# x ahead of the weight bits, a first stage on column halves, and two weight parts converted by VectorE and GpSimd

## The chip, the cores and the metric

The kernel runs on one core of a Trainium2 chip. The core has TensorE (PE in the profile; its weight loads are PEld), VectorE (DVE), ScalarE (ACT), GpSimd (POOL), and SyncE (SP), which here only issues DMAs. Sixteen DMA engines move data between HBM and the on-chip memory SBUF; TensorE writes into a second on-chip memory, PSUM, of eight banks. The metric is the device time of one execution in microseconds (us); lower is better. Times named "before" are for the kernel without the change.

## The reference

The reference filters a sequence in the frequency domain and puts the result through a two-layer network with a hard-swish:

```python
# x: (8, 3008, 256) float32; filt_r, filt_i: (1505, 256) float32
X = np.fft.rfft(x, axis=1)
F = (filt_r + 1j * filt_i)[None, :, :]
y = np.fft.irfft(X * F, n=3008, axis=1).astype(np.float32)
t = y.reshape(8 * 3008, 256)
h = t @ w_in                                  # w_in: (256, 2048)
g = h * np.clip(h + 3.0, 0.0, 6.0) / 6.0
out = (g @ w_out).astype(np.float32)          # w_out: (2048, 256)
```

Both weights come as 8-byte floating-point numbers. [...]

## The kernel before, in words

**The transform.** 3008 is 47 times 64, and the transform is done in stages of small matrix products. For every batch: a first stage over 47 rows, a second stage (`b_unit`) over 64, the product with the filter (`f_unit`), the way back in two stages (`bi_unit`, then `n_five`, `n_unit`, or `n_first` and `direct` for the very first tokens). Between the stages the data changes its layout. Batches 1 to 7 go through HBM for that (`z_tmp`, `g_tmp`), and their work is spread over the main stage, in which the two weight products (`plain_up` and `plain_down` in the first block of 512 tokens, `up_1` to `up_5` and `down` in the others) fill TensorE. Batch 0 is different: it has to be done first, before the main stage has anything to work on, and it has its own path.

**Batch 0, first stage.** x of batch 0 is loaded by six DMAs (`x0_load`, line 406) into the upper end of the tile `w_all`, which later holds the weights. `x0` is seen as 32 columns j of 256 values. `a0_unit(j)`, called eight times, takes four j; for each half `dh` of the 256 values it makes four products into one PSUM bank, with 128 columns of x as the stationary operand and the 128 columns of the table `start` as the moving one, of which 96 (4 times KH) are then copied out. The copies (`copy`, lines 413 and 415) go to `zt(0)` by ScalarE and to `zt(1)` by VectorE, save for j of 8 and 12, where ScalarE does both. `bank(0)` hands out four PSUM banks in turn.

**Batch 0, second stage.** The loop over c from 0 to 5 is the heart of the change's neighbourhood. `turn(c)` transposes with TensorE and copies with ScalarE. Each round has two units i (2c and 2c+1): `b_unit` is two products on TensorE, `f_unit` three VectorE operations that read the product in PSUM and a filter tile in SBUF. After the round's units come `turn(c + 1)`, `bi_unit(0, 2c - 2)` with two ScalarE copies (line 587) and `g_store(0, 2c - 2)` (line 631): two DMAs issued by GpSimd itself, in the order of its other work. The copies of `bi_unit` go to a buffer that a store reads: units 0, 4 and 8 use the pool `t1p` with two buffers (the tile `y0` of the last round takes one of them between units 4 and 8), units 2 and 6 the single buffer of `t3p`. In the last round `g0_first` issues the stores of unit 8 on ScalarE's and SyncE's queues (line 625). `first_load` (line 663) reads back what the stores wrote, in two parts; `direct` (line 732) and `n_first` make the first tokens from it.

**The order of DMAs.** Loads are issued by SyncE in the order in which the program calls them, and no more than some eight are under way at once. `table_load(0, c)` loads the filter rows and the table of round c (five DMAs, 0.8 MB); rounds 0 and 1 have their own tiles, rounds 2 to 5 go into space that x0 leaves free after the first stage. `load_bits(n)` loads the raw words of weight parts up to part n - 1 (one DMA, 512 KB each). `wi` is a table that `bi_unit` reads.

**The conversion of a weight part.** `w_abs(i)` is a pair of ScalarE operations (lines 323 and 324): the absolute value of the upper word into a tile `high`, and the lower word as a scaled float. `w_conv(i)` is three VectorE operations on the upper word (lines 333, 335, 337), or four where `w_abs` was not called. `w_conv_2(i)` multiplies, adds, and masks tiny numbers, three VectorE operations (lines 354 or 356, 358, 361; line 349 too without `w_abs`). Part 0 is converted in the first stage, after `a0_unit(4)`; parts 1, 2 and 3 after the second stage (`convert(3)`), with `w_abs(3)` behind `n_first`; the other twelve in halves in the first block of the main stage (`convert_half`), each in a step of its plan.

**Order of instructions.** The program order is the order on every engine (`manual_schedule`); semaphores are set where one engine's data is another's input or where a buffer is reused.

Of the kernel before, what the change touches and what calls it, by code (L numbers as in the profile page):

```python
# [10 lines left out]
FP32 = mybir.dt.float32  # L11
I32 = mybir.dt.int32
AXT = mybir.ActivationFunctionType
ALU = mybir.AluOpType
# [15 lines left out]
KH = 24  # L30
X0, XR = 16, 112
NF = N // 2 + 1
P = 128
# [5 lines left out]
HC = NC // 2  # L39
# [6 lines left out]
FB = 2  # L46
# [137 lines left out]
def kernel(  # L184
# [9 lines left out]
    nc = tc.nc  # L194
# [5 lines left out]
    wi_d = nc.inline_tensor(wi_np, name="wi_t").ap()  # L200
# [10 lines left out]
    def pool(name, bufs, **kw):  # L211
        return ctx.enter_context(tc.tile_pool(name=name, bufs=bufs, **kw))
# [4 lines left out]
    sp = pool("sp", 2)  # L217
# [3 lines left out]
    rp = pool("rp", 2)  # L221
# [3 lines left out]
    op = pool("op", 2)  # L225
# [12 lines left out]
    wi = const.tile([P, 4, NC], FP32, name="wi")  # L238
# [10 lines left out]
    st = {}  # L249

    def raw(src, row, ap):
        return bass.AP(tensor=src.tensor, offset=src.offset + row * D, ap=ap)


    def table_load(b, c):
        if b == 0 and c >= FB:

            at = x0_at(1536 * (c - FB), 1536)
            t, wb = at[:, 0:1024].rearrange("p (k d) -> p k d", k=TC), at[:, 1024:].rearrange("p (k m) -> p k m", k=TC)
        else:  # L260

            t, wb = ft[(b * NT + c) % FB], wa[:, ds(c % FB * TC * P, TC * P)].rearrange("p (k m) -> p k m", k=TC)
        st["ft", b, c] = t
        if b:

            for src, p0 in ((filt_r, 0), (filt_i, HALF)):
                for r in range(2):
                    o = p0 + 32 * r
                    nc.sync.dma_start(t[o:o + 16, :, :].rearrange("p k d -> p (k d)"),
                                      raw(src, c * TC + NA * r, [[2 * NA * D, 16], [1, TC * D]]))  # L270
                    nc.sync.dma_start(t[o + 16:o + 32, :, :],
                                      raw(src, NA * (2 - r) - c * TC, [[2 * NA * D, 16], [-D, TC], [1, D]]))
            return
        for src, p0 in ((filt_r, 0), (filt_i, HALF)):
            nc.sync.dma_start(t[p0:p0 + 32, :, :].rearrange("p k d -> p (k d)"),
                              raw(src, c * TC, [[NA * D, 32], [1, TC * D]]))
            nc.sync.dma_start(t[p0 + 32:p0 + 64, :, :], raw(src, NA - c * TC, [[NA * D, 32], [-D, TC], [1, D]]))
        nc.sync.dma_start(wb, wb_d[:, ts(c, TC), :])
        st["wb", b, c] = wb
# [10 lines left out]
    def w_part(i):  # L290
        i = PART[i]
        p = i // 2
        if i % 2 == 0:
            cols = ts(p, 256)
            src = moe_w_in[:, cols].bitcast(I32)
            return src.rearrange("(a p) d -> p a d", p=P), w_in[p][:, 0:4, :].rearrange("p (a j) m -> p a (j m)", a=2)
        src = moe_w_out[ts(p, 2 * P), :].bitcast(I32)
        return src.rearrange("(a p) d -> p a d", p=P), w_out[p][:, 0:4, :].rearrange("p (a j) m -> p a (j m)", a=2)
# [18 lines left out]
        q.dma_start(t.rearrange("p (a d) -> p a d", a=2), w_part(i)[0])  # L317
        st["bits", i] = t

    def w_abs(i):  # L320
        words = st["bits", i].rearrange("p (n two) -> p n two", two=2)
        st["high", i] = sp.tile([P, 512], FP32, name="s1")
        nc.scalar.activation(out=st["high", i], in_=words[:, :, 1].bitcast(FP32), func=AXT.Abs)
        nc.scalar.activation(out=words[:, :, 0].bitcast(FP32), in_=words[:, :, 0].bitcast(mybir.dt.uint32), func=AXT.Copy, scale=2.0 ** -32)


    def w_conv(i):
        words = st.pop(("bits", i)).rearrange("p (n two) -> p n two", two=2)
        lo, hi = words[:, :, 0], words[:, :, 1]
        big, rest = (yp.tile([P, 2, D], FP32, name="y").bitcast(I32).rearrange("p a n -> p (a n)") for j in range(2))  # L330
        v = nc.vector
        st["conv", i] = big, rest, lo, hi
        v.tensor_scalar(out=big, in0=hi, scalar1=3, scalar2=0x3FFFFFFF,
                        op0=ALU.logical_shift_left, op1=ALU.bitwise_and)
        v.scalar_tensor_tensor(out=big, in0=hi, scalar=top_c, in1=big,  # L335
                               op0=ALU.bitwise_and, op1=ALU.bitwise_or)
        v.tensor_scalar(out=rest, in0=big, scalar1=23, scalar2=23,
                        op0=ALU.logical_shift_right, op1=ALU.logical_shift_left)
        if ("high", i) not in st:
            v.tensor_scalar(out=lo, in0=lo, scalar1=9, scalar2=0x3F800000,  # L340
                            op0=ALU.logical_shift_right, op1=ALU.bitwise_or)

    def w_conv_2(i):
        big, rest, lo, hi = st.pop(("conv", i))
# [55 lines left out]
    def x0_at(o, n):  # L400
        return w_all.rearrange("p a b c m -> p (a b c m)")[:, ds(NP * 14 * P - HC * D + o, n)]

    x0 = x0_at(0, HC * D).rearrange("p (j d) -> p j d", d=D)
# [4 lines left out]
    def zt(dh):  # L408
        return (xn.rearrange("p a c n -> p (a c n)"), xs.rearrange("p i j d -> p (i j d)"))[dh]

    def copy(dve, to, ps):
        if dve:
            nc.vector.tensor_copy(out=to, in_=ps)
        else:
            nc.scalar.activation(out=to, in_=ps, func=AXT.Copy)

    def a0_unit(j):
        for dh in range(2):
            ps = bank(0)
            for u in range(4):  # L420
                nc.tensor.matmul(ps[:, ts(u, P)], x0[0:XR, j + u, ts(dh, P)], st["start"][0:XR, ts(1, P)],
                                 start=True, stop=True)
            copy(dh and j not in (8, 12), zt(dh).rearrange("p (n j) -> p j n", j=HC)[:, j:j + 4, :],
                 ps.rearrange("p (j n) -> p j n", j=4)[:, :, 0:4 * KH])

    def turn(c):
# [139 lines left out]
    def y_unit(b, i):  # L566
        s1, s2 = st["y", b, i]
        if b == 0 and i % 2 == 0:
            st["y0"] = t1p.tile([P, 2, 2, D], FP32, name="t1")
        y = yp.tile([P, 2, D], FP32, name="y") if b else st["y0"][:, i % 2, :, :]  # L570
        re, im = slice(0, HALF), slice(HALF, P)
        nc.vector.tensor_tensor(out=y[re], in0=s1[re], in1=s1[im], op=ALU.subtract)
        nc.vector.tensor_tensor(out=y[im], in0=s2[re], in1=s2[im], op=ALU.add)
        st["y", b, i] = y
# [62 lines left out]
    for b in range(B):  # L637
# [4 lines left out]
        n = 0  # L642
# [120 lines left out]
    def strips(ps, w, x, **kw):  # L763
        for o in range(0, P, STRIP):
            nc.tensor.matmul(ps[ds(o, STRIP)], w[:, ds(o, STRIP)], x, skip_group_check=True, **kw)  # L765
# [214 lines left out]
    with tc.manual_schedule():  # L980
# [17 lines left out]
        def load_bits(most):  # L998
            nonlocal loaded
            while loaded < most and w_before(loaded) < done:  # L1000
                w_load(loaded, nc.sync)
                loaded += 1

        def convert(n):
            nonlocal done
            for i in range(n):
                w_conv(done)
                w_conv_2(done)
                done += 1
# [10 lines left out]
            load_bits(NCONV)  # L1020

        nc.scalar.activation(out=zero[:, 0:1], in_=half_c, func=AXT.Copy)
        nc.scalar.dma_start(wi, wi_d)
        ps = psU.tile([P, 512], FP32, name="al")

        def keep_warm(n):
# [1 line left out]
                nc.tensor.matmul(ps, zero[:, P:2 * P], zero, start=True, stop=True)  # L1028

        keep_warm(2)  # L1030
        for j, n, bits in (0, 4, 0), (4, 4, 0), (8, 8, 1), (16, 8, 1), (24, 4, 1), (28, 4, 1):
            x0_load(j, n)
            load_bits(bits)
        table_load(0, 0)
        load_bits(2)
        table_load(0, 1)
        for j in range(0, HC, 4):
            a0_unit(j)
            convert(j == 4)
        nc.gpsimd.memset(t4, 0.0)  # L1040
        for c in range(FB, NT):
            table_load(0, c)
        last = x0_at(HC * D - 2048, 3 * ND)
        nc.sync.dma_start(last, direct_d[:, 0:3, :].rearrange("p k n -> p (k n)"))
        load_bits(3)
# [5 lines left out]
        for c in range(NT):  # L1051
            for i in (2 * c, 2 * c + 1):
                b_unit(0, i)
                f_unit(0, i)
                if c == NT - 1:
                    y_unit(0, i)
            if c + 1 < NT:
                turn(c + 1)
            if c:
                bi_unit(0, 2 * c - 2)  # L1060
                (g0_first if c == NT - 1 else lambda i: g_store(0, i))(2 * c - 2)
            if c == 4:
                first_load(0, KH - 3 * TC)
        first_load(KH - 3 * TC, KH - TC)
        for i in 1, 2:
            w_abs(i)
        direct(NU - 2)
        direct(NU - 1)

# [8 lines left out]
            x_load(1, c)  # L1078
            load_bits(7 + c)
        w_abs(3)  # L1080
        convert(3)

        def wai_load():
            nc.sync.dma_start(wa[:, 528:], wa_d[:, 528:])
# [32 lines left out]
        for i in range(2, len(chunks)):  # L1117
# [7 lines left out]
            s0, s1 = ((k - 1) * NP + s for s in steps)  # L1125
# [63 lines left out]
        for i in range(len(items) + 1):  # L1189
            up = i < len(items)  # L1190
            k, p = items[min(i, len(items) - 1)]
# [98 lines left out]
```

## Time and profile before

| What | Value |
|---|---|
| time, median of 3 runs (lowest to highest) | 2609.06 us (2608.47 to 2609.44) |
| the profiled execution: span from first to last instruction | 2607.0 us |
| the same execution's own time | not listed apart from its span; the median stands 2.06 us above it |
| PE busy | 2591.8 us, 99% |
| DVE busy | 2053.9 us, 79% |
| ACT busy | 1295.6 us, 50% |
| POOL busy | 486.7 us, 19% |
| mean granted TensorE clock | 1.000 |
| first stage of batch 0, PE (L421) | 6.6 to 22.1 us |
| first product of the main stage (L765) | 64.2 us |

A line of the timeline or of a group names the engine, the source line (L421), the operation, the tiles it writes and reads, the shape, and how many records of it there are. A matrix product of 32-bit floats leaves two records. An entry in brackets is the time for which the engine stood idle before it, with the engine or DMA it had waited for. The chain of waits is followed back from the last instruction: at each step to what released it.

### The profile page before, as it was taken

The numbers are of one execution on the slowest core, as the hardware profiler recorded it, in microseconds if no ns is written. First come the engines' busy times: TensorE is split into PE (matmuls) and PEld (weight loads), VectorE is DVE, ScalarE is ACT, GpSimd is POOL, SyncE is SP. The second block draws the span as 40 slices with busy tenths as digits, with TensorE's granted clock in tenths as the row PEclk, the third lists the DMA queues.
The fourth block names the chain that finished last, engine by engine and source line by source line (L and its number), as shares of the span: only waits on it lengthen the run. The fifth ranks groups of instructions, "written<-read, shape, count | busy, mean of one in ns | idle before, by whom it ended". The sixth has DMA issues, their size and how long they took to land.

```text
span 2607.0 us, 86613 instructions
## 1 busy us (share of the span) xinstructions
PE 2591.8 (99%) x37708; PEld 2051.0 (79%) x37708; DVE 2053.9 (79%) x3611; ACT 1295.6 (50%) x2677; POOL 486.7 (19%) x711
## 2 busy tenths in 40 slices
PE   8999999999999999999999999999999999999999
PEld 6487777878778787788877888777877778888887
DVE  7978868888788877888778887788877888766666
ACT  4554454545545455444554444545445454455554
POOL 2242021121211202111031210311113120111110
PEclk9999999999999999999999999999999999999999
DMA  8732234112241132411224112331123321110000
GB/s 247 224 92 81 59 101 119 54 33 87 74 123 54 33 87 78 119 54 37 83 83 114 54 38 82 89 108 54 54 66 91 106 57 49 50 44 24 20 22 26
DMA packets 130834, 200.32 MB, mean 77 GB/s; under 512 B 21602, under 2 KB 97472, under 8 KB 130262
## 3 DMA queue, kind: packets, MB, share of 16 engines
q1 hardware_dynamic: 115165, 150.12, 20.4%
q0 software_dynamic: 14720, 44.16, 6.1%
q8 instruction: 296, 4.85, 0.8%
q14 instruction: 84, 0.69, 0.1%
q10 hardware_dynamic: 569, 0.50, 0.1%
HBM read 122.43 MB, written 83.98 MB: 79 GB/s over the span
## 4 chain that ended last, share of the span: by engine, by line
PE 94%; DVE 3%; DMA 2%; POOL 1%; issue 0%; ACT 0%; SPq 0%; POOLq 0%; DVEq 0%; ACTq 0%
PE po L765 43%; PE al L765 24%; PE be L765 18%; PE psn L705 2%; PE psf L540 1%; PE psf L481 1%; PE psf L600 1%; PE be L600 1%; POOL w_all L369 1%; PE be L481 1%; DVE g L818 1%; DMA g_tmp<-t 1%; PE psf L765 0%; DMA ft<-in_filt_i_dram 0%; DVE y L335 0%
## 5 line engine op out<-in xcount | busy, mean ns | idle before, releaser
L765 PEld LDWEIGHTS po<-w_all,g 128*64 128x64 f32 x20808 | 1232.5, 137 | 247.0 <-issue 12.4
L765 PE MATMUL po<-w_all,g 128*64 128x128 f32 (+1 forms) x20808 | 1407.0, 274 | 1.4 <-DVE g L818 0.7
L813 ACT ACTIVATE r<-h,half_c 128x512 f32<-128x512 f32 x736 | 531.0, 722 | 346.7 <-DVE h L794 334.7
L765 PE MATMUL al<-xt,w_all 128*64 128x256 f32 x4416 | 664.0, 379 | 0.4 <-POOL w_all L369 0.3
L818 DVE SCALAR_TENSOR_TENSOR g<-r,h 128x512 f32<-128x512 f32 x736 | 536.2, 730 | 144.6 <-ACT r L813 129.2
L765 PE MATMUL be<-xt,w_all 128*64 128x256 f32 x2944 | 442.6, 379 | 0.0
L794 DVE TENSOR_TENSOR h<-be,s 128x512 f32<-128x512 f32 x368 | 253.8, 690 | 131.3 <-PE be L765 102.2
L760 POOL TENSOR_TENSOR xt<-xn 128x256 f32<-128x256 f32 x184 | 150.7, 838 | 890.3 <-ACT xn L687 890.3
L765 PEld LDWEIGHTS be<-xt,w_all 128*64 128x64 f32 x2944 | 211.3, 137 | 106.5
L765 PEld LDWEIGHTS al<-xt,w_all 128*64 128x64 f32 x4416 | 278.9, 137 | 1.7 <-POOL w_all L369 1.4
L808 ACT ACTIVATE h<-al 128x256 f32<-128x256 f32 x368 | 141.4, 384 | 273.2 <-PE al L765 272.4
L826 DVE TENSOR_TENSOR g<-g 128x512 f32<-128x512 f32 x367 | 261.4, 712 | 12.6
L799 DVE TENSOR_TENSOR h<-al,s 128x256 f32<-128x256 f32 x368 | 156.0, 424 | 135.6 <-PE al L765 130.5
L789 ACT ACTIVATE s<-al 128x256 f32<-128x256 f32 x368 | 141.6, 385 | 207.2 <-PE al L765 207.1
L765 PE MATMUL al<-xn,w_all 128*64 128x256 f32 (+1 forms) x1536 | 240.1, 393 | 1.1 <-DVE g L818 0.7
L765 PE MATMUL be<-xn,w_all 128*64 128x256 f32 (+1 forms) x1536 | 236.4, 388 | 0.0
L780 ACT ACTIVATE s<-be 128x256 f32<-128x256 f32 x368 | 141.4, 384 | 170.1 <-PE be L765 170.1
L825 DVE TENSOR_TENSOR g<-g 128x256 f32<-128x256 f32 x367 | 165.5, 451 | 12.6
L779 ACT ACTIVATE s<-al 128x256 f32<-128x256 f32 x368 | 141.5, 384 | 59.1 <-PE al L765 59.1
L831 DVE TENSOR_TENSOR g<-g 128x256 f32<-128x256 f32 x367 | 161.7, 441 | 2.4
L765 PEld LDWEIGHTS be<-xn,w_all 128*64 128x64 f32 x1536 | 110.3, 137 | 62.3 <-issue 7.4
L506 POOL DMA_DIRECT2D z_tmp<-t x144 | 72.0, 508 | 321.4 <-ACT s L780 296.0
(162 smaller groups left out, 1766.6 us busy)
## 6 DMA issues: line engine op xcount, KB each, us to landing
t<-g_tmp SPq DMA_DIRECT2D x184, 120.0 KB
t<-z_tmp SPq DMA_DIRECT2D x42, 512.0 KB
g_tmp<-t POOLq DMA_DIRECT2D x68, 256.0 KB, 4.3
z_tmp<-t POOLq DMA_DIRECT2D x120, 144.0 KB, 3.7
o_tmp<-o SPq DMA_DIRECT2D x46, 256.0 KB
xs<-in_x_dram SPq DMA_DIRECT2D x60, 192.0 KB
ft<-in_filt_r_dram SPq DMA_DIRECT2D x168, 64.0 KB
ft<-in_filt_i_dram SPq DMA_DIRECT2D x168, 64.0 KB
```

The source lines that it names most:

```text
L760: nc.gpsimd.tensor_tensor(out=o, in0=x0, in1=x1, op=op_)
L765: nc.tensor.matmul(ps[ds(o, STRIP)], w[:, ds(o, STRIP)], x, skip_group_check=True, **kw)
L779: nc.scalar.activation(out=s[:, 0, :], in_=al, func=AXT.Copy)
L780: nc.scalar.activation(out=s5, in_=be[:, 1, :], func=AXT.Copy)
L789: nc.scalar.activation(out=s[:, 1, :], in_=al, func=AXT.Copy)
L794: nc.vector.tensor_tensor(out=st["h"][0].rearrange("p (a n) -> p a n", a=2), in0=be, in1=s, op=ALU.add)
L799: nc.vector.tensor_tensor(out=st["h"][1][:, 256:512], in0=al, in1=s5, op=ALU.add)
L813: nc.scalar.activation(out=r, in_=st["h"][i], func=AXT.Relu, bias=half_c, scale=1.0 / 6.0)
L818: nc.vector.scalar_tensor_tensor(out=st["g", k, p][:, o:o + 2, :].rearrange("p a n -> p (a n)"), in0=st["r", i], scalar=1.0, in1=st["h"][i ...
L825: v.tensor_tensor(out=g[:, G1, :], in0=g[:, G3, :], in1=g[:, G22, :], op=ALU.add)
L826: v.tensor_tensor(out=g[:, G3:G2 + 1:2, :], in0=g[:, G3:G1 + 1, :], in1=g[:, G11:G11 + 1, :].broadcast_to([P, 2, 256]), op=ALU.subtract)
L831: nc.vector.tensor_tensor(out=g[:, G4, :], in0=g[:, G12, :], in1=g[:, G2, :], op=ALU.subtract)
```

## The change

Three things change. First, the loads: all six DMAs of x go first, then the tables of rounds 0 and 1, then part 0's bits, then `wi` (on SyncE's queue, no longer ScalarE's); part 1's bits go behind table 3. Second, `a0_unit` uses `strips`: each product is made as two, with 64 stationary columns each, and the moving operand is cut to the 96 columns that are copied out; VectorE makes all copies of the second half. Third, parts 0 and 1 are no longer converted in the first stage and after the second, but in rounds 1 and 3 of the second stage: ScalarE's pair, VectorE's three operations, and a new function `w_conv_2g` with four GpSimd operations in place of VectorE's three. Their tile `high` comes from another pool. `convert(3)` becomes `convert(2)`.

```diff
-    def w_abs(i):
+    def w_abs(i, early=False):
         words = st["bits", i].rearrange("p (n two) -> p n two", two=2)
-        st["high", i] = sp.tile([P, 512], FP32, name="s1")
+        st["high", i] = rp.tile([P, 512], FP32, name="r", tag="r") if early else sp.tile([P, 512], FP32, name="s1")
...
-        nc.scalar.activation(out=words[:, :, 0].bitcast(FP32), in_=words[:, :, 0].bitcast(mybir.dt.uint32), func=AXT.Copy, scale=2.0 ** -32)
+        nc.scalar.activation(out=words[:, :, 0].bitcast(FP32), in_=words[:, :, 0].bitcast(mybir.dt.uint32), func=AXT.Copy,
+                             scale=2.0 ** (-52 if early else -32))
...
+    def w_conv_2g(i):
+        big, rest, lo, _ = st.pop(("conv", i))
+        rest, big, high, g = rest.bitcast(FP32), big.bitcast(FP32), st.pop(("high", i)), nc.gpsimd
+        two = lambda t: t.rearrange("p (a d) -> p a d", a=2)
+        g.tensor_tensor(out=rest, in0=lo.bitcast(FP32), in1=rest, op=ALU.mult)
+        g.tensor_tensor(out=rest, in0=rest, in1=big, op=ALU.add)
+        g.tensor_scalar(out=high, in0=high, scalar1=1.125 * 2.0 ** -15, scalar2=None, op0=ALU.is_ge)
+        g.tensor_tensor(out=w_part(i)[1], in0=two(high), in1=two(rest), op=ALU.mult)
...
             for u in range(4):
-                nc.tensor.matmul(ps[:, ts(u, P)], x0[0:XR, j + u, ts(dh, P)], st["start"][0:XR, ts(1, P)],
-                                 start=True, stop=True)
-            copy(dh and j not in (8, 12), zt(dh).rearrange("p (n j) -> p j n", j=HC)[:, j:j + 4, :],
+                strips(ps[:, ds(u * P, 4 * KH)], x0[0:XR, j + u, ts(dh, P)], st["start"][0:XR, ds(P, 4 * KH)],
+                       start=True, stop=True)
+            copy(dh, zt(dh).rearrange("p (n j) -> p j n", j=HC)[:, j:j + 4, :],
...
-        nc.scalar.dma_start(wi, wi_d)
...
-        for j, n, bits in (0, 4, 0), (4, 4, 0), (8, 8, 1), (16, 8, 1), (24, 4, 1), (28, 4, 1):
+        for j, n in (0, 4), (4, 4), (8, 8), (16, 8), (24, 4), (28, 4):
             x0_load(j, n)
-            load_bits(bits)
         table_load(0, 0)
-        load_bits(2)
         table_load(0, 1)
+        load_bits(1)
+        nc.sync.dma_start(wi, wi_d)
         for j in range(0, HC, 4):
             a0_unit(j)
-            convert(j == 4)
         nc.gpsimd.memset(t4, 0.0)
         for c in range(FB, NT):
             table_load(0, c)
+            load_bits(1 + (c > FB))
...
+            if c in (1, 3):
+                w_abs(done, True)
+                w_conv(done)
+                w_conv_2g(done)
+                done += 1
             if c + 1 < NT:
                 turn(c + 1)
...
-        for i in 1, 2:
-            w_abs(i)
+        w_abs(2)
...
-        convert(3)
+        convert(2)
```

`strips`, which the change now calls here too, cuts the stationary operand and the output in two:

```python
def strips(ps, w, x, **kw):
    for o in range(0, P, STRIP):          # STRIP = 64
        nc.tensor.matmul(ps[ds(o, STRIP)], w[:, ds(o, STRIP)], x, skip_group_check=True, **kw)
```

## The prediction

> **What bounds the kernel now.** I read the stage table first, then the chain of waits, then each engine's timeline in the stretch that the change touches. The page says that PE is busy 99% of the span. From about 126 us on nothing here is edited, and PE runs without gaps, so the change can only move the moment at which that stream starts. The stretches of 20 us (columns: stretch, length, busy PE, PEld, DVE, ACT, POOL, granted clock, DMA share, GB/s):
>
> ```profile
> 0.00:20.00 20.00, 16.98 (x115) 14.91 (x116) 8.88 (x16) 9.13 (x12) 8.55 (x9) 1.00 0.93 253
> 20.00:40.00 20.00, 18.60 (x109) 13.43 (x109) 16.46 (x24) 7.87 (x15) 2.42 (x4) 1.00 0.96 253
> 40.00:60.00 20.00, 18.89 (x84) 10.26 (x84) 18.45 (x29) 7.39 (x14) 2.27 (x4) 1.00 0.67 216
> ```
>
> DVE is half idle in the first stretch and nearly full in the next two; POOL is nearly free after 20 us; the DMA engines are saturated until 40 us and beyond (the table by 2 us has share 1.04 at 46 to 48 us, and 0.51 at 48 to 50). Then the chain from 42 us to the first product of the main stage (start, length, what):
>
> ```profile
> 42.65 0.53 POOL g_tmp L631
> 43.18 6.58 DMA g_tmp<-t
> 49.87 0.37 ACT t L587
> 50.98 4.56 DMA g_tmp<-t
> 55.56 2.31 DMA g_tmp<-t
> 58.19 3.34 DMA t<-g_tmp
> 61.62 1.86 PE psn L765 x40
> 64.22 1.93 PE al L765 x7
> ```
>
> So what starts the main stage is neither DVE nor PE. It is a store of g issued on POOL's queue: `g_store(0, 4)`. ACT's copy for `bi_unit(0, 8)` reuses the buffer of that store (pool t1p has two) and waits for its landing; `g0_first`, `first_load` and `n_first` follow. The PE timeline shows a second path from the same copy:
>
> ```profile
> 6.59 15.48 PE L421 MATMUL po<-p,w_all 112*128 112x128 f32 x128
> 51.16 1.81 PE L732 MATMUL psn<-w_all,t 128*128 128x470 f32 x4 [1.02 <-ACT t L587]
> 61.62 1.85 PE L765 MATMUL psn<-wai,t 128*64 128x94 f32 x40 [0.80 <-DMA t<-g_tmp]
> ```
>
> `direct` (L732) needs the banks which that copy frees, and arrives at `n_first` only 0.80 us before the DMA does. Both paths hang on the landing at 49.8 us.
>
> **The change part by part.**
>
> *a0 on halves.* 64 products of two records and 128 columns become 128 strips, 256 records of 96 columns. The nearest row is `n_first`, also 64-column halves with new weights each: 40 records of 94 columns take 1.65 us (61.62 to 63.27), 41 ns each, 42 ns for 96 columns. 256 x 42 ns = 10.8 us. Before, evictions come every 0.895 us for 16 banks, but the first ends at 8.54 and the second at 9.60: PE is at half rate until about 8.6 us. That costs 1.2 us before and some 0.9 after. The chunk j = 4 to 7 lands about 9.2 (SP waited for x until 9.73 before; some 0.5 us of wi traffic leaves): 0.2 of wait. a0 ends after 12.0 us instead of 15.5: **3.5 us earlier**. Ends: 4.7 earlier without those two waits; 6 later if halves do not run side by side (256 records at 0.895/8 x 96/128 us). I take the `n_first` row, it is the same form. The evictions fit: 0.84 us each on ACT and DVE per 1.35 us pair.
>
> *Loads.* x (3.1 MB, six DMAs) no longer shares its time with bits 0 (0.5 MB, issued between its third and fourth chunk), and both bits and wi (1.2 MB in all) leave the way of table 1. At 253 GB/s that is 4.6 us: the table that PE waited for at 27.65 (0.59 us, chain 27.5) lands near 22.9 and is wanted at 23.6 (27.06 - 3.5). wi, on SP's queue behind bits 0 and off ACT's, has 5.5 MB up to its end against 6.0 that landed at 27.5, so about 25.4; `bi_unit(0, 0)` wants it at 26.9. If that cover fails, each us late is a us on bi and its store. Bits 0 lands about 25 and is wanted by ACT at 24.3 and by DVE at 30.4. Bits 1 takes the place in bytes that table 3 had (b6 used that at 36.95 without a wait), wanted by DVE at 40.6. SP issues as many DMAs as before, tables 2 to 5 no later. Each costed at nothing under these covers.
>
> *The old conversion of part 0* (4.4 us of DVE, 12.07 to 16.45) sat in DVE's idle time before `po L421` (10.9 us): its removal earns nothing. ACT gives two copies back to DVE: nothing. The full conversion of part 1 (3.84 us) leaves DVE after 54.68, but part 3's second half waits for ACT's pair behind `n_first` (L354 at 65.64, 1.61 us idle) and hswish L818 waits behind that, in both versions. So this earns nothing either: `n_first` decides.
>
> *The new halves on DVE.* Three operations a part:
>
> ```profile
> 54.68 0.43 DVE L333 TENSOR_SCALAR y<-bits 128x512 int32<-128x512 int32 x1
> 55.15 0.75 DVE L335 SCALAR_TENSOR_TENSOR y<-bits,top_c,y 128x512 int32<-128x512 int32 x1
> 55.93 0.43 DVE L337 TENSOR_SCALAR y<-y 128x512 int32<-128x512 int32 x1
> 154.01 0.69 DVE L794 TENSOR_TENSOR h<-be,s 128x512 f32<-128x512 f32 x1 [1.41 <-ACT s L789]
> 98.99 1.10 DVE L358 SCALAR_TENSOR_TENSOR y<-y 128x512 f32<-128x512 f32 x1
> ```
>
> With the hand-over that is 1.6 us a part, in a DVE stream of 2.14 us per unit without gaps (25.36 to 42.49 for eight). The last two rows show DVE beside a busy POOL: with an operand in PSUM 0.69 us, undisturbed; with both in SBUF 1.10 instead of 0.69. `f_unit` reads PSUM, so GpSimd's new work should not slow it. DVE starts at 25.36 - 3.5 = 21.9, ends unit 3 at 30.4, part 0 at 32.0, unit 7 at 40.6, part 1 at **42.2**. ACT's pair (two of 0.66) fits into its idle 1.8 to 2.5 us per round. The waits of f4 and f8 behind these halves reach bi(4) and bi(8), neither before its old moment.
>
> *The new halves on GpSimd*, and what stands behind them. POOL is in order, and in rounds 1 and 3 the four operations come ahead of that round's `g_store`. So stores 0 and 2 wait for part 0, and stores 4 and 6 for part 1:
>
> ```profile
> 122.50 0.89 POOL w_all L369 x2
> 346.16 1.54 POOL L760 TENSOR_TENSOR xt<-xt 128x256 f32<-128x256 f32 x2
> 42.65 1.13 POOL L631 DMA_DIRECT2D g_tmp<-t  x2 [3.53 <-ACT t L587]
> DMA to landing us min/median/max: 2.9/6.8/9.7
> ```
>
> 128 columns take 0.44 us, 256 take 0.72 on their median and 0.77 in this row; on that line 512 take 1.29. Three of these and the `is_ge` (between DVE's 0.43 for a like operation and 1.29; I take 0.75 as it has one input) are **4.6 us**. Ends for a part: 2.1 (DVE's own 0.69 thrice, and no is_ge) and 10 (four at twice the slowest 256-column row, 1.24). I take the middle, the row of the same operation. Part 0: 32.0 to 36.7, then stores 0 and 2 until 39; the last store lands some 6.8 later at 45.3, and bi(6), which reuses its buffer, copies before 47.12 as it did. Part 1: 42.2 to 46.8. **Store 4 is issued at 46.8 instead of 42.65**, its second DMA at 47.4. It then finds less traffic: its 6.58 us fell into a saturated stretch that ends at 48; here 0.5 MB of stores less are ahead. I take 4.2, between the least of L631 (2.9) and the old 6.58: landing 51.6 instead of 49.8, **1.8 us late**. ACT's copies for bi(8), two DMA issues of `g0_first` and the conversion pair of part 2 are queued behind that wait. The DMA path then repeats: `n_first` 1.8 later. PE's path has its 0.80 of slack: 1.0 later. So **+1.8**.
>
> PE idles about 4.5 us ahead of `direct` (bi(8) done near 48.5, copy over near 53), where it idled 1.02. The rows above have PE at half rate from its first product at 3.02 to about 8.6, none after a later gap. Bounds from these: nothing, or 2.8 us (half of 5.6) on PE's path, less 0.8 of slack. I take nothing for the sum. The Trainium skill ("TensorE: Matmul & The Clock Gate", "What's actually happening") has the clock halved after an idle window of about 3.4 us and whole again after as much work. This speaks against the change; by it `direct` would lose about 1.7 us and the sum would be an estimated +2.7. No row here shows it.
>
> The Trainium skill ("GPSIMD Engine Reference", "Engine selection") also advises against elementwise work on GpSimd, about half as fast for two inputs; the rows here give 1.29 against 0.69. By it alone the move loses; by the timeline POOL's time is free, and what costs is the queue behind it.
>
> Sum: +1.8 us. The page's execution has a span of 2607.0, 2.1 under the median of 2609.06; I take that remainder as unchanged. **2610.9 us**.
>
> **The rivals.**
> 1. *Stores not late* (chance 0.22). If GpSimd needs only some 2.5 us a part, or the store lands in 3 us, the earlier a0 gets through: landing at 42.2 + 2.5 + 0.6 + 3 = 48.3, 1.5 early, 2607.6; with all of a0's gain 3.5 early, 2605.6. For it: a nearly idle POOL and the minimum of 2.9. Against it: the measured rows of POOL.
> 2. *POOL's queue decides alone* (0.20; the other side). Place: `g_store(0, 4)` behind part 1. At 8 us a part (strided words, two-input operands, near the contended rows) it lands 3.4 later than forecast: +5.2, 2614.3. From 8 us on it is slower by over 0.2%; at 10 us 2616.3. Against it: contended rows belong to DVE operations with two SBUF inputs, which are few here.
> 3. *Halves don't overlap* (0.04): a0 6 us later instead of 3.5 earlier, 2620. The `n_first` row speaks against it.
>
> **How the numbers follow.** The forecast has 0.54, with its own range 2608.5 to 2613.5 (store landing 2.9 to 6.6, clock 0 to +2). 0.2% is 5.2 us, about what a measurement of this kernel can tell: below 2603.8 only the best of rival 1 with a0's 4.7 reaches, 0.06; above 2614.3 lie most of rival 2, rival 3 and a little of the forecast, 0.20; 0.74 between. Range 2605.2 to 2616, leaving out 0.08 below and 0.12 above.
>
> **What would show it.** Right: L421's group as x256 in about 11 to 12 us, DVE's first `f_unit` near 21.9; POOL's four operations at 32 and 42 us, and store 4 issued near 47; the chain through `g_tmp` with ACT L587 at 51 to 52; `psn L765` at 63 to 64. Wrong: store 4 before 44; f_units over 0.75 us beside POOL; PE waiting for x or for table 1; main products starting before 62 or after 67; anything different after 126 us.

## The result and the profile after the change

| | before | after |
|---|---|---|
| time, median of 20 runs each | 2607.95 us (2607.26 to 2609.44) | 2612.40 us (2611.39 to 2615.00) |
| ratio, 95% interval | | 1.0018 (1.0011 to 1.0024) |
| span of the profiled execution | 2607.0 | 2611.2 |
| first stage's last copy ends, `turn(0)` goes on | 22.96 | 21.98 |
| store 4 (`g_store(0, 4)`) issued by POOL | 42.65 | 50.55 |
| first product of `n_first` | 61.62 | 66.24 |
| first hswish on VectorE (L818, now L828) | 67.81 | 72.43 |

The kernel became 4.5 us slower. All of it is there when the main stage starts: from the first hswish to the end the span has 2539.2 us before and 2538.8 after. The chain of waits of the changed kernel, in the same stretch as before (start, length, what; the line numbers are about ten higher):

```profile
50.61 0.53 POOL g_tmp L641
51.13 3.75 DMA g_tmp<-t
54.99 0.36 ACT t L597
56.11 4.08 DMA g_tmp<-t
60.20 2.20 DMA g_tmp<-t
62.72 3.43 DMA t<-g_tmp
66.24 1.86 PE psn L775 x40
```

The chain has the same steps as before. Only its first is 8 us late, and the landing is 2.8 us shorter, so that ACT's copies for bi(8), which is `bi_unit(0, 8)`, begin at 54.99 instead of 49.87. POOL's timeline shows why the store is late:

```profile
42.53 0.69 DVE L573 TENSOR_TENSOR h<-po,w_all 64x512 f32<-64x512 f32 x1
44.60 0.43 DVE L338 TENSOR_SCALAR y<-y 128x512 int32<-128x512 int32 x1
45.17 1.29 POOL L348 TENSOR_TENSOR y<-bits,y 128x512 f32<-128x512 f32 x1 [2.42 <-issue]
46.53 1.26 POOL L349 TENSOR_TENSOR y<-y 128x512 f32<-128x512 f32 x1
47.77 1.48 POOL L350 TENSOR_SCALAR r<-r 128x512 f32<-128x512 f32 x1
49.34 1.27 POOL L351 TENSOR_TENSOR w_all<-r,y 128x512 f32<-128x512 f32 x1
50.55 1.21 POOL L641 DMA_DIRECT2D g_tmp<-t  x2
```

VectorE ends its last `f_unit` of round 3 and, at 45.03, the three operations of part 1; GpSimd works from 45.17 to 50.6; only then does the store go. PE in the first stage, and after its long wait:

```profile
6.72 3.85 PE L775 MATMUL po<-p,w_all 112*64 112x96 f32 x64
10.73 6.71 PE L775 MATMUL po<-p,w_all 112*64 112x96 f32 x152 [0.16 <-DMA w_all<-in_x_dram]
19.22 1.87 PE L775 MATMUL po<-p,w_all 112*64 112x96 f32 x40 [1.78 <-issue]
51.58 3.68 PE L594 MATMUL psf<-s,wi 128*64 128x512 f32 x8 [4.59 <-ACT t L597]
55.64 2.30 PE L742 MATMUL psn<-w_all,t 128*128 128x470 f32 x4 [0.38 <-ACT t L597]
```

The gap of 1.78 us in the first stage, in which PE waits for nothing that the profile shows, was not in the forecast; the halved clock was, but was put at nothing in its sum. bi(8) takes 3.68 us where it took 1.94 in the kernel before:

```profile
48.21 1.94 PE L584 MATMUL psf<-s,wi 128*64 128x512 f32 x8
```

PE's idle time of 4.59 us stands ahead of bi(8), which needs ACT's copies of bi(6); these came only at 50.93. The stretches of 2 us of the changed kernel have the granted clock in the column ahead of the DMA share:

```profile
48.00:50.00 2.00, 0.00 (x0) 0.00 (x0) 1.96 (x3) 0.00 (x0) 1.92 (x2) 0.94 0.73 281
52.00:54.00 2.00, 2.00 (x6) 0.47 (x4) 1.90 (x4) 0.02 (x1) 1.13 (x2) 0.50 0.92 215
56.00:58.00 2.00, 2.00 (x7) 0.93 (x6) 1.77 (x4) 0.08 (x1) 0.00 (x0) 0.85 0.75 150
```

### The profile page after: what moved, and what is told of

It reads as the page before. It is cut to its first block, busy times and chain, and to the rows that moved or that the text cites. A ratio compares the mean times of both kernels' runs of the same rounds, so it can differ in the third digit from the quotient of the medians.

```text
span 2611.2 us, 86875 instructions
## 1 busy us (share of the span) xinstructions
PE 2590.9 (99%) x37836; PEld 2047.7 (78%) x37836; DVE 2050.6 (79%) x3605; ACT 1295.1 (50%) x2677; POOL 497.9 (19%) x719
## 4 chain that ended last, share of the span: by engine, by line
PE 97%; DVE 1%; DMA 1%; issue 0%; ACT 0%; POOL 0%; SPq 0%; POOLq 0%; DVEq 0%; ACTq 0%
PE po L775 45%; PE al L775 25%; PE be L775 18%; PE psn L715 2%; PE psf L550 1%; PE psf L491 1%; PE psf L610 1%; PE be L610 1%; PE be L491 1%; DMA g_tmp<-t 0%; PE po L559 0%; PE psf L775 0%; DMA w_all<-in_x_dram 0%; PE psf L464 0%; PE psn L775 0%
## 5 line engine op out<-in xcount | busy, mean ns | idle before, releaser
L828 DVE SCALAR_TENSOR_TENSOR g<-r,h 128x512 f32<-128x512 f32 x736 | 535.6, 729 | 144.7 <-ACT r L823 129.6
L818 ACT ACTIVATE h<-al 128x256 f32<-128x256 f32 x368 | 141.4, 384 | 274.0 <-PE al L775 273.3
```

Source lines behind the costliest of these rows:

```text
L828: nc.vector.scalar_tensor_tensor(out=st["g", k, p][:, o:o + 2, :].rearrange("p a n -> p (a n)"), in0=st["r", i], scalar=1.0, in1=st["h"][i ...
```

## The experiments

Each group ran on one chip, beside the kernel before (2608.03, 2608.24 and 2608.11 us in the three groups). The theory: store 4 waits on POOL's queue behind part 1, and what follows keeps its distance from it. Rivals: GpSimd's or VectorE's extra work costs wherever it stands; the halved clock is what costs; the loads or the halves cost.

### The changed kernel again

> The changed kernel once more, beside the others on the same chip. Expected as measured: about 4.4 us over the kernel before (0.17%), store 4 issued at 50.5 us, first product of n_first at 66.2 us.

2613.62 us, ratio 1.0021 (1.0011 to 1.0030). Store 4 goes at 50.41 as before, but in this profile the clock was still halved when `direct` began:

```profile
55.85 3.50 PE L742 MATMUL psn<-w_all,t 128*128 128x470 f32 x4 [3.10 <-ACT t L597]
59.94 2.71 PE L742 MATMUL psn<-w_all,t 128*128 128x470 f32 x4
68.06 1.85 PE L775 MATMUL psn<-wai,t 128*64 128x94 f32 x40
```

`n_first` no longer waits for a DMA and comes 1.8 us later than in the first profile (68.06 against 66.24); the spans differ by 1.9. From the start of `direct` to the end of the last product ahead of `n_first` PE took 9.7 us in the kernel before, 9.8 in the first profile and 12.3 in this one; some 0.8 us of that was slack. So the halved clock cost about nothing in the one profile and 1.8 us in the other. That fits a part of the kernel's spread, 2611.4 to 2615.0.

### The store ahead of GpSimd's work

```diff
             if c in (1, 3):
                 w_abs(done, True)
                 w_conv(done)
-                w_conv_2g(done)
-                done += 1
...
                 (g0_first if c == NT - 1 else lambda i: g_store(0, i))(2 * c - 2)
+            if c in (1, 3):
+                w_conv_2g(done)
+                done += 1
```

> The changed kernel with the four GpSimd operations of a round placed behind that round's g_store. Queue theory (what costs is store 4 waiting on POOL behind part 1): store 4 is issued near 41.5 us instead of 50.5, ACT's copies for bi(8) start at 48.5 to 50 instead of 55, n_first at 60.5 to 61.5, and the time falls by 5 us against the changed kernel, to 0.5 to 1.5 us under the kernel before. Rival (GpSimd's work itself, or VectorE's added 3.2 us, costs wherever it stands): the time stays at 2611 to 2613.

2609.87 us, ratio 1.0005 (0.9996 to 1.0014): 3.75 us under the changed kernel beside it, and the ten runs of the one (2607.55 to 2611.11) do not meet those of the other (2611.39 to 2614.89). The order on POOL's queue alone carries most of the loss; GpSimd does the same work. The gain is less than the 5 us expected, and the profile (of the slowest of the ten runs) shows what comes next:

```profile
41.20 2.37 POOL L641 DMA_DIRECT2D g_tmp<-t  x4
51.18 1.12 ACT L597 ACTIVATE t<-psf 128x512 f32<-128x512 f32 x2 [1.05 <-DMA g_tmp<-t]
53.21 0.69 DVE L583 TENSOR_TENSOR t<-h 64x512 f32<-64x512 f32 x1
54.00 1.81 PE L742 MATMUL psn<-w_all,t 128*128 128x470 f32 x4 [2.37 <-issue]
```

POOL issues stores 2 and 4 in one row (x4), and the copies for bi(8) are over at 52.3. But `direct` starts at 54.00, when VectorE ends `y_unit(0, 10)` at 53.90. VectorE's added work, some 3.5 us, hidden behind the late store in the changed kernel, is on the path here. VectorE was a limit of `direct` already in the kernel before:

```profile
50.37 0.69 DVE L573 TENSOR_TENSOR t<-h 64x512 f32<-64x512 f32 x1
```

There `y_unit(0, 10)`, which `direct` reads, ended at 51.06 and `direct` began at 51.16, while ACT's first copy for bi(8), begun at 49.87, took 0.6 us. In this profile the first stage also ended 1.0 us later than in the first profile of the changed kernel, since its last 40 records ran at half clock.

### The conversion alone, on the kernel before

The edit is the changed kernel's third part (parts 0 and 1 put together from their words in rounds 1 and 3, with `w_conv_2g`, and `convert(2)`), with loads and first stage as before.

> The kernel before with the third part of the change alone: parts 0 and 1 converted in rounds 1 and 3 on VectorE and GpSimd; loads and first stage as before. Queue theory: VectorE's half of part 1 ends at 45.9 us, four operations of 5.4 us, store 4 at 51.4, landing near 55.7 against 49.8: 5.5 to 6 us slower than before, 2613.5 to 2614. If the slowdown came from the new first stage or the new order of loads: 2608 to 2610.

2615.76 us, ratio 1.0028 (1.0017 to 1.0039), 7.7 us over before, where 5.5 to 6 were expected.

```profile
52.18 2.34 POOL L641 DMA_DIRECT2D g_tmp<-t  x4
57.60 3.50 PE L742 MATMUL psn<-w_all,t 128*128 128x470 f32 x4 [5.55 <-ACT t L597]
```

Store 4 is 9.5 us late, 0.8 later than expected (PE stood 1.24 us for x in the first stage here), and `direct` starts at half clock (0.50 from 56 to 60 us). The conversion's place costs more than the whole change; the loads and the halves together give some 2 us of it back (2613.62 against 2615.76).

### PE kept busy through its wait

```diff
+            if c == NT - 1:
+                busy = psU.tile([P, 512], FP32, name="al")
+                for i in range(4):
+                    nc.tensor.matmul(busy, st["start"][:, 0:P], zt(0)[:, 0:512], start=True, stop=True)
             if c:
                 bi_unit(0, 2 * c - 2)
```

> The changed kernel with four products of 512 columns that nobody reads in PE's idle time ahead of bi_unit(0, 8) (47 to 51 us), so that the clock is not halved. Queue theory: the granted clock stays at 1.00, bi(8) takes 1.9 instead of 3.7 us, but the copies still wait for store 4 at 54.9: n_first within 0.3 us of 66.2, time within 0.5 us of the changed kernel. Clock theory (the halved clock from 49 to 56 us costs): n_first 2 us or more earlier and the time 2 us lower.

2612.98 us, ratio 1.0018 (1.0009 to 1.0028), 0.6 us under the changed kernel on the same chip, within the spread of both.

```profile
51.16 1.94 PE L594 MATMUL psf<-s,wi 128*64 128x512 f32 x8 [0.41 <-ACT t L597]
65.16 1.84 PE L775 MATMUL psn<-wai,t 128*64 128x94 f32 x40 [0.63 <-DMA t<-g_tmp]
```

The clock stayed at 1.00 from 46 to 64 us and bi(8) took 1.94 us again, and the kernel is still 4.95 us over before: the halved clock is not the main cause. `n_first` came 1.08 us earlier than in the first profile of the changed kernel, neither within 0.3 us nor by 2; 0.47 us of that was there when store 4 went, at 50.08. The share of the clock in the median is not told apart from nothing.

### Full width with 96 columns

```diff
-                strips(ps[:, ds(u * P, 4 * KH)], x0[0:XR, j + u, ts(dh, P)], st["start"][0:XR, ds(P, 4 * KH)],
-                       start=True, stop=True)
+                nc.tensor.matmul(ps[:, ds(u * P, 4 * KH)], x0[0:XR, j + u, ts(dh, P)], st["start"][0:XR, ds(P, 4 * KH)],
+                                 start=True, stop=True)
```

> The changed kernel with the first stage's products on full width (128 stationary columns) but with 96 moving columns: 128 records in place of 256. Code theory (PE stands still at 17.4 us for 1.8 us because its next block of instructions has not come): by the rate of 0.895 us for 8 records of 128 columns the stage takes the same 10.8 us of products, with half the instructions, and the gap of 1.8 us goes: turn(0) starts near 19.5 us instead of 21.3, and the time is 1.5 to 2 us under the changed kernel. Halves theory (the halves bring the gain of the first stage): the stage takes as long as with 128 columns, turn(0) near 22, time 0.5 to 1 us over the changed kernel.

2614.58 us, ratio 1.0025 (1.0015 to 1.0034).

```profile
6.58 15.49 PE L431 MATMUL po<-p,w_all 112*128 112x96 f32 x128
```

128 records with 96 columns take 15.49 us; with 128 columns they took 15.48. The moving columns cost nothing at full width, so my claim that the stage would be as fast with half the instructions falls: the halves bring the gain. Weight loads overlap in both forms: one of 128 columns takes 192 ns and a record comes every 121 ns, one of 64 takes 137 ns and a record comes every 44. What sets the pace at full width is not shown.

### Where PE's gap belongs

```diff
         keep_warm(2)
+        for i in range(24):               # 4 in the second kernel
+            nc.tensor.matmul(ps[:, 0:16], zero[:, P:2 * P], zero[:, 0:16], start=True, stop=True)
```

> The changed kernel with 24 products of 16 columns behind the first two dummy products, 96 instructions for PE in all with the weight loads, which nobody reads. Code theory: the gap without a releaser comes 48 records earlier in the first stage, after 168 records instead of 216, near 15.4 us. Data theory (a chunk of x or something else that happens at a time): the gap stays behind record 216, at 17.4 us.

Inconclusive, 2623.95 us in one run. The 24 products took 10.26 us, 214 ns a record, at a slow rate: a weight load took 333 ns instead of 192, although the column of the granted clock reads 1.00 there. The first stage then ran 256 records in 13.42 us without a gap, which neither theory had. The run shows something else: its first stage ended 9.1 us later than the changed kernel's, and store 4 went 9.2 us later (59.71 against 50.55).

> The changed kernel with four products of 16 columns behind the first two dummy products (16 instructions of PE with the weight loads, 1.7 us). If PE's gap without a releaser belongs to a place in its instruction stream counted from the start, it comes after 208 records of the first stage; if it belongs to the product itself (its data, its bank), after 216; if to a moment, near 17.4 us whatever the record; if PE is then late enough, there is none.

2614.12 us in one run.

```profile
8.24 10.17 PE L775 MATMUL po<-p,w_all 112*64 112x96 f32 x208
19.82 2.20 PE L775 MATMUL po<-p,w_all 112*64 112x96 f32 x48 [1.41 <-issue]
```

The gap comes after 208 records, eight earlier, a microsecond later by the clock. Eight records with as many weight loads are the 16 instructions added ahead. So, by this one run, it belongs to a place in PE's instruction stream, counted from the start; not to x, to a bank, or to a moment. In all six kernels that have the changed first stage at its old place in the stream and x first, the gap stands behind record 216 and lasts 1.0 to 1.9 us. The place alone is not enough: the halves alone on the kernel before (next section) have the same stage at the same place and no gap there; PE had stood 2.99 us for x and took 65 ns a record. In the profiles read for it, one transfer of 16 KB on the instruction queue falls within some 2 us ahead of the gap, while the DMA engines are saturated (share 1.07 from 16 to 18 us). That PE waits for code is the reading that fits; that this transfer is PE's own is not shown. The Trainium skill ("Runtime: NRT & Kernel Launch", "Instruction fetch mechanics") has an engine's instructions refilled in blocks of 256 and the fetch hidden as a rule. That the gap keeps to a count of instructions agrees with the first, though no run shows that the count is a multiple of 256; the 1.0 to 1.9 us, if they are a fetch, disagree with the second in this stretch.

### The halves alone, on the kernel before

The edit is `strips` with 96 columns in `a0_unit` of the kernel before, nothing else.

> The kernel before with the second part of the change alone: halves and 96 columns in the first stage; loads and conversions as before. Code theory: the stage is held by the same gap and by x, whose fourth chunk lands at 14.5 us behind bits 0: turn(0) at 20.5 to 21.5 instead of 22.1 to 23.0, the table of round 1 at 27.5 as before, so the time 0 to 0.6 us under before. If the first stage set the end by itself: 3 us under before.

2609.38 us, ratio 1.0003 (0.9994 to 1.0013): no change is shown, where 0 to 0.6 us under before was expected.

```profile
10.80 2.86 PE L765 MATMUL po<-p,w_all 112*64 112x96 f32 x64 [0.21 <-DMA w_all<-in_x_dram]
16.65 8.31 PE L765 MATMUL po<-p,w_all 112*64 112x96 f32 x128 [2.99 <-DMA w_all<-in_x_dram]
```

With bits 0 still among the chunks of x, a faster PE only reaches the fourth chunk early, stands for 3 us, and the clock is halved (0.50 from 16 to 22 us; the profile is of the slowest of the ten runs). The halves need the new order of loads.

### Both edits, full width and the store first

> The changed kernel with both edits: GpSimd's operations behind the store, and full width with 96 columns. If both theories hold the gains add up: store 4 near 40 us, n_first at 59.5 to 61, time 1 to 3 us under the kernel before. The landing of store 4 is then bounded by the DMA engines, which are saturated until some 46 us, so less than the sum is expected. If the first stage's gain is off the path: as the store moved alone.

2610.31 us, ratio 1.0013 (1.0002 to 1.0024), not the 1 to 3 us under before that the sum would have given: the full width gives nothing, and VectorE's work holds `direct` at 53.76 (`y_unit(0, 10)` ends at 53.66). One of the ten runs took 2624.11 us and draws the ratio up; the medians are 2.1 us apart.

### Nothing on GpSimd

```diff
-            if c in (1, 3):
-                w_abs(done, True)
-                w_conv(done)
-                w_conv_2g(done)
-                done += 1
...
-        w_abs(2)
+        w_abs(0)
+        w_abs(1)
...
+        convert(1)
+        w_abs(2)
         for c in range(2):
             x_load(1, c)
             load_bits(7 + c)
+        convert(1)
         w_abs(3)
         convert(2)
```

> The changed kernel without the conversions in rounds 1 and 3: parts 0 to 3 are converted by ScalarE and VectorE behind the second stage, nothing on GpSimd; loads and halves stay. Queue theory: the stores go out as in the kernel before, about 1 us earlier (the first stage's measured gain), n_first at 60.5 to 61; but VectorE has four whole parts of 3.84 us from 53.7 on and hswish comes at 69 to 70 instead of 67.8: time 1 to 2.5 us over before, bounded by VectorE, not by the stores. If loads and halves themselves cost: n_first at 63 or later.

2613.51 us, ratio 1.0021 (1.0012 to 1.0030).

```profile
41.31 1.13 POOL L641 DMA_DIRECT2D g_tmp<-t  x2 [3.53 <-ACT t L597]
60.59 1.84 PE L775 MATMUL psn<-wai,t 128*64 128x94 f32 x40 [0.61 <-DMA t<-g_tmp]
64.61 0.69 DVE L364 TENSOR_TENSOR y<-g,y 128x512 f32<-128x512 f32 x1 [1.92 <-ACT g L324]
70.61 0.69 DVE L828 SCALAR_TENSOR_TENSOR g<-r,al 128x512 f32<-128x512 f32 x1
71.36 3.19 PE L775 MATMUL al<-xn,w_all 128*64 128x512 f32 x8 [4.51 <-DVE g L828]
```

The stores and `n_first` are 1.0 to 1.3 us earlier than in the kernel before. That is the share of loads and halves. Hswish then comes at 70.61, 2.8 us late, past the 69 to 70 worked out: VectorE has four whole parts ahead of it, and for 1.92 us of that it waits for ScalarE's pair of part 2, which this edit puts behind `n_first`. How much would be left with the pair earlier, no run shows. PE idles 4.5 us there and goes on at half clock (0.50 from 72 to 74 us), and the time is 5.4 us over before, more than expected. So with x first, part 0 has to go somewhere: its bits were issued at 2.14 us in the kernel before and are issued at 18.53 in the changed one, so the idle time of VectorE in the first stage is no longer to be had.

### One part later, and both parts later

In the first kernel GpSimd's half of part 0 goes behind store 4, and part 1 is converted (both halves) behind the second stage; ScalarE's pair of part 3 goes ahead of `n_first`.

```diff
-            if c in (1, 3):
-                w_abs(done, True)
-                w_conv(done)
-                w_conv_2g(done)
-                done += 1
+            if c == 1:
+                w_abs(0, True)
+                w_conv(0)
...
+            if c == 3:                    # behind g_store(0, 4)
+                w_conv_2g(0)
+                done += 1
...
         first_load(KH - 3 * TC, KH - TC)
+        w_abs(1, True)
+        w_conv(1)
+        w_conv_2g(1)
+        done += 1
         w_abs(2)
+        w_abs(3)
```

> The changed kernel with GpSimd's half of part 0 behind store 4 (round 3), part 1 converted as a whole behind the second stage (both halves), and ScalarE's pair of part 3 ahead of n_first. Queue theory with VectorE as the next limit: no store waits for GpSimd, VectorE's own delay ahead of direct falls from 3.2 to 1.6 us, store 4 near 41, copies of bi(8) at 48.5 to 50, direct at 51 to 52, n_first at 61 to 62, hswish 0.7 us closer to it: time 0 to 1.5 us under the kernel before. Rival (GpSimd's work disturbs VectorE wherever it stands): no better than with the store first, 1.5 to 2 us over before.

2607.25 us against 2608.11, ratio 0.9998 (0.9990 to 1.0007).

```profile
41.21 1.13 POOL L641 DMA_DIRECT2D g_tmp<-t  x2 [3.54 <-ACT t L597]
50.08 1.81 PE L742 MATMUL psn<-w_all,t 128*128 128x470 f32 x4 [1.11 <-ACT t L597]
60.45 1.85 PE L775 MATMUL psn<-wai,t 128*64 128x94 f32 x40 [0.72 <-DMA t<-g_tmp]
66.48 0.69 DVE L828 SCALAR_TENSOR_TENSOR g<-r,al 128x512 f32<-128x512 f32 x1
```

With all three parts of the change in this form the loss is gone: `n_first` comes 1.2 us and hswish 1.3 us earlier than in the kernel before. VectorE is the next limit here too: `y_unit(0, 10)` ends at 49.98, 0.1 us ahead of `direct`, and beside GpSimd's work on part 1 two of its operations take 1.67 and 1.68 us (L336 and L368, 0.75 and 0.69 else). It is the fastest kernel of the study by its median, but the interval holds no change. In the second kernel both parts are converted behind the second stage, with the same edit for part 3.

> The changed kernel with both parts converted behind the second stage (VectorE's and GpSimd's halves), and ScalarE's pair of part 3 ahead of n_first. VectorE has no extra work ahead of direct: direct at 49.5 to 51, n_first at 59.5 to 61. Then GpSimd works from 54 to 66 beside VectorE operations with two SBUF operands, which take 1.1 instead of 0.7 us in the kernel before: parts 2 and 3 end near 67, hswish there: time 0.5 to 1.5 us under before if that contention holds, 2 to 3 us under if it does not.

2614.30 us, ratio 1.0025 (1.0015 to 1.0034), the wrong side.

```profile
56.46 1.68 DVE L336 SCALAR_TENSOR_TENSOR y<-bits,top_c,y 128x512 int32<-128x512 int32 x1
59.29 0.83 DVE L338 TENSOR_SCALAR y<-y 128x512 int32<-128x512 int32 x1 [1.15 <-POOL y L349]
62.13 1.51 DVE L334 TENSOR_SCALAR y<-g 128x512 int32<-128x512 int32 x1 [2.01 <-DMA xt<-in_moe_w_in_dram]
73.17 0.69 DVE L828 SCALAR_TENSOR_TENSOR g<-r,al 128x512 f32<-128x512 f32 x1
```

Here that rival, that GpSimd's work disturbs VectorE, holds: beside 11.6 us of GpSimd work the two-operand L336 takes 1.68 instead of 0.75 us and the one-operand L334 1.51 instead of 0.43. I had reckoned with 1.1. VectorE also waits 1.15 us for a buffer that GpSimd still reads (pool yp has three). hswish comes at 73.17, although `n_first` was at 61.60. GpSimd's place matters: beside `f_unit`, which reads PSUM, VectorE's operations stay at 0.69 us in the changed kernel.

## Why the prediction was right, and where its terms were off

The mechanism held. It put the loss at store 4 behind part 1 on POOL's queue, with the same chain after it; the run with the store first takes 3.75 of the 5.6 us back by order alone, and the trace of that run puts VectorE's added work next. The forecast was +1.8 us, the result +4.45; `n_first` came 4.6 us later. So the change was mis-sized by 2.65 us. That 2610.9 us lies only 1.5 us under the result is in part luck: the three runs of the kernel before on which it stood have a median 1.1 us above that of the twenty. The events came some 2 to 4 us later than the signs of being right had them, and two signs of being wrong came: the main products start at 68.93, after 67, and PE waited for x, by 0.16 us. By its own steps:

- *a0 on halves*: forecast 3.5 us, measured 1.0. This term was mis-sized by 2.5 us, and it is the largest miss. 256 records at 42 ns was close (152 in 6.71 us, 44 ns; the full-width run shows that the halves make it). Missing were the gap of 1.78 us at record 216, for which the trace of before had no row, and some 0.7 us in slower rates, waits and a later start.
- *Loads*: covered, as forecast; PE no longer waits for the table of round 1. Alone, the halves would have met the fourth chunk of x.
- *VectorE's halves*: 1.6 us each forecast; 1.7 and 1.8 measured, and `f_unit` undisturbed. With the hand-over to GpSimd, VectorE's stream was some 0.45 us longer than forecast.
- *GpSimd*: 4.6 us forecast, 5.4 measured. The three two-input operations took 1.26 to 1.30 each (1.29 forecast from the 128- and 256-column rows; the median of the latter is 0.73, not 0.72); `is_ge`, with one input, took 1.48 to 1.5 instead of 0.75. The choice "one input, so half" was wrong: 0.8 us.
- *Landing of the store*: 4.2 forecast, 3.75 measured.
- These sum to what is seen at ACT's copy for bi(8): 1.8 + 2.5 + 0.45 + 0.8 - 0.45 = 5.1, against 5.12 (54.99 and 49.87). `n_first` came only 4.62 later, as the two transfers of `g0_first` and the load behind them took 9.71 us in the chain instead of 10.21. A landing as late as this, 3.3 us past the forecast, is what the second rival had (3.4); it came at 5.4 us a part, not 8, because a0's gain was missing.
- *The paths*: `direct` was read as waiting for ACT's copy alone. In the kernel before it waited for VectorE's `y_unit(0, 10)`, which ended 0.1 us ahead of it. In the changed kernel that ended at 52.91, well ahead of `direct` at 55.64, so the reading did no harm here; it is what the run with the store first met.
- *bi(6)*: wrong. Its copies were to come before 47.12 and came at 50.93, after a wait of 6.99 us for store 2. Store 4 was later still, so the chain did not hang on it, but PE's idle time did, which so stood ahead of bi(8) and not, as forecast, ahead of `direct`.
- *The clock*: taken at nothing in the sum, with bounds of 0 and 2 us. It was halved, as the Trainium skill ("TensorE: Matmul & The Clock Gate", "What's actually happening") had it for an idle window of about 3.4 us, here 4.59. The loss on the path from `direct` on that was estimated from that page, 1.7 us, lies between those of the two profiles: some 0.15 in the first, 2.6 in the second, of which 0.8 was slack. A shorter gap was once followed by the half clock too, and one of 3.39 us was not (last section).
- *The old conversion earns nothing*: right for part 1; n_first to hswish is 6.19 us in both. For part 0 its removal earned nothing too, but the run without GpSimd shows what else it does: it leaves a whole part to be converted later.
- *Rivals*: stores not late did not happen; POOL's queue decided, but at 5.4 us a part, under the 8 us at which that rival began; the halves do overlap.

## What to carry to other kernels

A nearly idle engine is free only as long as nothing stands behind the new work on its queue: before work is given to an engine that also issues DMAs, list those DMAs and who waits for their landing, and put the work behind the store that a chain hangs on. An engine can also get slower beside the new work: VectorE's two-operand L336 went from 0.75 to 1.68 us beside GpSimd, while `f_unit`, with one operand in PSUM, stayed at 0.69; look which operands the neighbour's operations read at that moment. And a stage that gets shorter should be checked for what it runs into next, the data, the code and the clock, before its whole gain is booked. When the first wait of an engine is shortened, the second one counts: here VectorE's `y_unit(0, 10)` ended 0.1 us ahead of `direct` already in the kernel before.

## What the runs showed of the hardware that was not expected

- PE stood still for 1.0 to 1.9 us at a fixed count of its instructions, when these were short (44 ns a record) and the DMA engines full (share 1.07). Sixteen instructions more ahead moved the gap by exactly eight products' records. Where PE took 65 ns a record behind a wait of 2.99 us, there was no gap.
- At full width a 32-bit product of 96 columns took as long as one of 128 (15.49 and 15.48 us for 128 records); as two halves of 64 stationary columns it took 44 ns a record, with twice the records, instead of 121.
- GpSimd's one-input comparison (1.48 us for 512 columns) was slower than its two-input multiply (1.27 to 1.30).
- VectorE beside GpSimd's two-input operations: 1.68 instead of 0.75 us with two operands in SBUF, more than the 1.10 against 0.69 us of the kernel before; unchanged with one operand in PSUM. L364, with two operands in SBUF, kept 0.69 us in the run with one part later, although 0.5 us of it (from 59.48) fell beside GpSimd's comparison.
- The clock was halved around PE gaps of 3.0, 3.45, 3.6 and 4.5 to 6.0 us and once around a gap of 1.87 us, but not by one of 1.78 us in the same place of another run, nor by 2.4 and 2.6 us elsewhere, nor by one of 3.39 us. The two rows are of the run with the store first (clock 0.50 from 20 to 22 us) and of the full-width run (1.00 from 50 to 56 us):

```profile
18.89 3.22 PE L775 MATMUL po<-p,w_all 112*64 112x96 f32 x40 [1.87 <-issue]
51.36 1.94 PE L594 MATMUL psf<-s,wi 128*64 128x512 f32 x8 [3.39 <-ACT t L597]
```
